# W1 pieces of two batches in shared tile groups, in the banks of the first matmul, and a wider spread of work at the start

## The chip, the cores and the metric

The kernel runs on one core of a Trainium2 chip. The metric is the device time of one execution in microseconds (us); smaller is better. Five engines matter: PE (TensorE, with PEld its weight loads), DVE (VectorE), ACT (ScalarE), POOL (GpSimd) and SP, which here only issues DMAs.

## The reference, cut to what matters

```
# x: (8, 8, 512, 64), state: (8, 8, 32, 64): batch, head, row, width
a     = softmax(x @ state^T / 8);   xread = a @ state      # 512 tokens per batch
a2    = softmax(state @ x^T / 8);   sread = a2 @ x         # 32 tokens per batch
tok   = concat([xread, sread], rows), heads side by side   # 8 x 544 tokens, 512 wide
out   = silu(tok @ w_in) @ w_out                           # w_in 512x2048, w_out 2048x512
```

## The kernel before

The kernel doesn't form `xread`. For each batch it makes W1 = state @ w_in, head by head (256 state rows by 2048 columns), and then multiplies the attention weights with W1. Numbers of `ft` count the 16 slices of 128 hidden columns, `tt` the 4 token tiles of a batch.

```
def w1_mms(b, cols, new=bank):      # one piece: 512 columns of W1, two PSUM banks
    for f, n in cols:
        for hg in range(2):
            pss[f, hg] = new([128, 512], FP32, "ps_w1")
        for s in range(4):
            for hg in range(2):     # 8 matmuls, each in a 64x32 tile of the array
                nc.tensor.matmul(pss[f, hg][ds(32 * s, 32), 0:n], stT[...], w_in_sb[...],
                                 tile_position=(r, 32 * s), ...)

def w1_out(b, cols, engs, pss, at=0):   # eviction: PSUM f32 -> SBUF bf16
    for f, n in cols:
        for hg in range(2):
            copy(engs[hg], W1[b][:, hg, ds(f + at, n)], pss[f, hg][:, ds(at, n)])

# G1(k), emitted by upto(): two 128x512 matmuls W1 x aT into a bank "h1" (two of them),
#   then ACT: g = silu(h).   G2(b, tt, ft): one matmul, out[tt] += g[ft] x w_out[ft]
```

The eight PSUM banks in batch 0 are: o0, o1, a0, a1 for the four outputs; a2, a3 for W1; and two "h1" banks through which all G1 pass in turn. The trace shows PE starting its matmuls in program order, so a G1 that waits for its bank holds up everything behind it. The loop of batch 0:

```
    banks[:] = ["a2", "a3"]
    W0 = {2: (512, 512), 6: (1024, 512), 10: (1536, 512)}
    LEAD0 = [2, 2, 2, 2, 2, 3, 2, 3, 3, 2, 2, 4, 4]
    F3 = 3
    ready = 4
    for ft in range(NFT - 2):
        upto(min(ft + LEAD0[min(ft, 12)], ready))       # G1 ahead of G2
        if ft in W0:
            w1_cols(0, [W0[ft]], both)                  # both = (DVE, ACT)
            ready = sum(W0[ft]) // 128
        ...
        if ft in (5, 9):
            w1_chunks(1, ({5: 0, 9: 1}[ft],), both)     # W1 of batch 1
        ... # ft 11: cast x of batch 1; ft 12: three G2 of tile 3, transposes of x
        for tt in range(4 if ft < F3 else 3):
            G2(0, tt, ft)
    ... # scores and softmax of batch 1, between them the rest of G2;
    ... # near the end the last two W1 pieces of batch 1, in one group
```

The `keep_busy` matmuls at the start are filler: nothing reads their results. Tile 3 has fewer G2 interleaved in the loop (F3); its other G2 are filler for the softmax of batch 1.

The softmax here doesn't subtract the row's maximum and nothing guards it: scores larger than these inputs give would overflow.

Of the kernel before, what the change touches and what calls it, by code (L numbers as in the profile page):

```python
# [25 lines left out]
NFT = DF // 128  # L26
# [15 lines left out]
def kernel(  # L42
# [84 lines left out]
    def cast_x(b, eng, c0=0, nc_=4, h0=0, nh=H):  # L127
        if b < 2:
            x_nat[b] = padded(b)
        elif b not in x_nat:  # L130
            x_nat[b] = xpool.tile([128, 4, 4, 128], BF16, tag="x_nat", name=f"x_nat{b}")
        copy(
            eng,
            x_nat[b][:, ds(c0, nc_), ds(h0 // 2, nh // 2), :].rearrange(
                "p c k (u d) -> p c k u d", u=2
            ),
            x_f[b % 2][:, ds(h0, nh), ds(c0, nc_), :].rearrange("p (k u) c d -> p c k u d", u=2),
        )
# [12 lines left out]
    def load_w_out(g0, n):  # L151
        nc.gpsimd.dma_start(w_out_sb[:, ds(g0, n), :], wout_re[:, ds(g0, n), :])  # L152

    def copy(eng, dst, src):
        if eng is nc.scalar:
            nc.scalar.activation(dst, src, func=COPY, bias=0.0)  # L156
        else:
            eng.tensor_copy(dst, src)  # L158


    def keep_busy(n, pool, tag):
        ps = pool.tile([128, 512], FP32, tag=tag, name="ps_busy")
        for _ in range(n):
            nc.tensor.matmul(  # L164
                ps[:], busy[:, 0:128], busy[:], start=True, stop=True, skip_group_check=True
            )
# [76 lines left out]
    def pe_transpose_x(b, hg, nb=2, new=bank, engs=(nc.vector, nc.scalar), only=None):  # L243
        if b not in xT:
            xT[b] = xtpool.tile([128, 4, 4, 128], BF16, tag="xT", name=f"xT{b}")
        m = 4 // nb
        for u in range(nb) if only is None else only:
            ps = new([128, m, 2, 128], BF16, "ps_xt")
            for i in range(m):
                for j in range(2):  # L250
                    nc.tensor.transpose(  # L251
                        ps[:, i, j, :],
                        x_nat[b][:, m * u + i, 2 * hg + j, :],
                        ident[:],
                    )
            copy(engs[u], xT[b][:, ds(m * u, m), ds(2 * hg, 2), :], ps[:])
# [9 lines left out]
    o_tags = ["o0", "o1"]  # L266
    new_o = lambda sh, dt, nm: psO.tile(sh, dt, tag=o_tags.pop(), name=nm)
    cast_x(0, nc.scalar, 2, 2, 4, 4)
    cast_x(0, nc.gpsimd, 0, 2, 4, 4)
    pe_transpose_x(0, 0, 2, new_o, (nc.vector, nc.vector))  # L270

    st_x = pers.tile([128, 8, B, 4, 2, 2], BF16)

# [116 lines left out]
            aT[b][:, hg, :, :], an[b, hg][:].rearrange("p c s n -> p (c s n)")  # L390
        )

    def pe_transpose_a(b, hg, eng, new=bank, c0=0, n=4):
        ps = new([128, n, 128], BF16, "ps_at")
        for c in range(n):
            nc.tensor.transpose(ps[:, c, :], an[b, hg][:, c0 + c, :, :], ident[:])
        copy(eng, aT[b][:, hg, ds(c0, n), :], ps[:])


    xm_ps = {}  # L400
# [48 lines left out]
    def w1_mms(b, cols, new=bank):  # L449
        pss = {}  # L450
        if b not in W1:
            W1[b] = wpool.tile([128, 2, DF], BF16, tag="W1", name="W1")
# [5 lines that stand above are left out]
                    h = HEAD_OF_SLOT[hg][s]  # L458
                    r = 64 * (h % 2)
                    nc.tensor.matmul(  # L460
                        pss[f, hg][ds(32 * s, 32), 0:n],
                        stT[ds(r, 64), b, h // 2, s % 2, :],
                        w_in_sb[ds(r, 64), h // 2, ds(f, n)],
                        start=True,
                        stop=True,
                        tile_position=(r, 32 * s),
                        skip_group_check=True,
                    )
        return pss

    def w1_out(b, cols, engs, pss, at=0):
# [4 lines that stand above are left out]
    def w1_cols(b, cols, engs, new=bank):  # L476
        w1_out(b, cols, engs, w1_mms(b, cols, new))

    def w1_chunks(b, fbs, engs):
        w1_cols(b, [(512 * fb, 512) for fb in fbs], engs)  # L480
# [83 lines left out]
    def store(b, tt, eng):  # L564
        o = opool.tile([128, DM], FP32, tag="o_sb", name="o_sb")
        copy(eng, o[:], outs[tt][:])
        if b < B:
            nc.sync.dma_start(out_re[ds(136 * b, 128), tt, :], o[:])
        else:
            nc.sync.dma_start(out_sread[ds(512, 32), ds(4 * tt, 4), :], o[:])  # L570
# [21 lines left out]
    def upto(k):  # L592
        while done[0] < min(k, (B + 1) * NFT):
            emit_G1(done[0])
            done[0] += 1

    new_h = lambda sh, dt, nm: psH.tile(sh, dt, tag="h1", name=nm)
    keep_busy(1, psH, "h1")
    scores(0, 0)
    exps(0, 0)  # L600
    keep_busy(1, psH, "h1")
    pe_transpose_x(0, 1, 2, new_h, (nc.vector, nc.scalar))
    norm(0, 0)
    scores(0, 1, 2)
    exps(0, 1)
    norm(0, 1, ((nc.vector, 0, 4),), 2)
    pss0 = w1_mms(0, [(0, 128)])
    nc.scalar.activation(warm[:], busy[:, 0:1], func=SILU, bias=0.0)
    w1_out(0, [(0, 128)], (nc.scalar, nc.scalar), pss0)
    load_w_in(1024)  # L610
    load_w_out(8, 4)
    load_w_in(1536)
    for hg in range(2):
        load_x(1, 4 * hg, 4)
    load_w_out(12, 4)
    load_states()
    load_x(2)
    for i in range(3):
        ones_beside_x(i, nc.gpsimd)
    keep_busy(3, psH, "h1")  # L620
    pss0 = w1_mms(0, [(128, 384)])
    keep_busy(2, psH, "h1")
    new_o = lambda sh, dt, nm: psO.tile(sh, dt, tag=o_tags.pop(), name=nm)
    o_tags[:] = ["o0", "o1"]
    for c in (0, 2):
        pe_transpose_a(0, 0, nc.scalar, new_o, c, 2)
    for c in (0, 2):
        pe_transpose_a(0, 1, nc.vector, bank, c, 2)
    upto(1)
    w1_out(0, [(128, 128)], (nc.vector, nc.vector), pss0)  # L630
    w1_out(0, [(128, 256)], (nc.vector, nc.vector), pss0, 128)
    upto(2)




    banks[:] = ["a2", "a3"]
    turn[0] = 0
    W0 = {2: (512, 512), 6: (1024, 512), 10: (1536, 512)}
    LEAD0 = [2, 2, 2, 2, 2, 3, 2, 3, 3, 2, 2, 4, 4]  # L640
    F3 = 3
    ready = 4
    for ft in range(NFT - 2):
        upto(min(ft + LEAD0[min(ft, 12)], ready))
        if ft in W0:
            w1_cols(0, [W0[ft]], both)
            ready = sum(W0[ft]) // 128
        if ft == 4:
            place_one_state(1, transpose_one_state(st1_n), nc.vector)
        if ft in (5, 9):  # L650
            w1_chunks(1, ({5: 0, 9: 1}[ft],), both)
        if ft == 11:
            for hg in range(2):
                cast_x(1, nc.vector, 0, 4, 4 * hg, 4)
            load_x(3)
        if ft == 12:
            nc.scalar.activation(warm[:], busy[:, 0:1], func=EXP, bias=0.0)
            for i in range(F3, F3 + 3):
                G2(0, 3, i)
            pe_transpose_x(1, 0, 1, engs=(nc.vector,))  # L660
            pe_transpose_x(1, 1, 1, engs=(nc.vector,))
        for tt in range(4 if ft < F3 else 3):
            G2(0, tt, ft)
    F3 += 3
    banks[:] = ["a2", "a3", "a0", "a1"]
    turn[0] = 0
    scores(1, 0, new=new_h)
    scores(1, 1, new=new_h)
    exps(1, 0)
    exps(1, 1)  # L670
    for tt in (0, 2, 1):
        G2(0, tt, 14)
        G2(0, tt, 15)
        if tt != 1:
            store(0, tt, nc.scalar)
    nc.scalar.activation(warm[:], busy[:, 0:1], func=SILU, bias=0.0)
    norm(1, 0)
    norm(1, 1, ((nc.vector, 0, 4),))
    tail_tags = ["a2", "a3", "a0", "o0"]

    def tail_bank(shape, dtype, name):
        tag = tail_tags.pop(0)
        return (psO if tag == "o0" else psA).tile(shape, dtype, tag=tag, name=name)

    for ft in range(F3, NFT):
        if ft == 12:
            pe_transpose_a(1, 0, nc.vector, new_h)
        if ft == 14:
            pe_transpose_a(1, 1, nc.vector, new_h)
            store(0, 1, nc.vector)  # L690
            cols = [(1024, 512), (1536, 512)]
            pss1 = w1_mms(1, cols, tail_bank)
            w1_out(1, cols, (nc.vector, nc.vector), pss1)
            for i in (2, 3):
                for c in range(4):
                    cast_x(i, nc.gpsimd, c, 1)
            transpose_states()
            transpose_x(2)
            upto(NFT + 2)
        G2(0, 3, ft)  # L700
    upto(NFT + 3)
    store(0, 3, nc.vector)

# [100 lines left out]
```

## Time and profile before

| | before |
|---|---|
| median time | 216.54 us (3 runs, 216.5 to 217.24) |
| profiled span | 214.5 us |
| PE busy | 208.0 us, 97% |
| PE's share of the chain that ended last | 87% |
| PE clock granted | 1.0 |

The head of the page of the kernel before, and the chain that ended last:

```profile
span 214.5 us, 3893 instructions
PE 208.0 (97%) x1575; PEld 96.8 (45%) x1575; DVE 76.7 (36%) x170; ACT 139.5 (65%) x244; POOL 39.4 (18%) x61
...
PE 87%; DVE 4%; POOL 3%; ACT 3%; issue 1%; POOLq 0%
```

PE bounds the kernel. Its busy share can't tell how much is left, though: a 128x512 matmul is drawn as 0.38 us long while the next one starts 0.216 us after it, so idle time of up to 0.16 us behind a matmul is drawn as work. Start times tell more. This is the timeline of PE in batch 0 of the kernel before; the columns are start, duration of the merged stretch, engine, line, operation, output<-inputs, array tile, operand size, count, and in brackets the idle time ahead with what ended it:

```profile
12.03 0.60 PE L514 MATMUL h<-aT,W 128*128 128x512 bf16 x2
12.47 0.59 PE L555 MATMUL o<-w_out_sb,g 128*128 128x512 bf16 x2
...
14.83 0.59 PE L514 MATMUL h<-aT,W 128*128 128x512 bf16 x2
15.35 0.41 PE L460 MATMUL ps_w<-w_in_sb,stT 64*32 64x512 bf16 x8
15.69 0.61 PE L555 MATMUL o<-w_out_sb,g 128*128 128x512 bf16 x2
...
27.27 0.38 PE L555 MATMUL o_a<-w_out_sb,g 128*128 128x512 bf16 x1
27.70 1.04 PE L514 MATMUL h<-aT,W 128*128 128x512 bf16 x4
28.99 0.59 PE L514 MATMUL h<-aT,W 128*128 128x512 bf16 x2 [0.25 <-ACT g L546]
...
37.61 0.63 PE L460 MATMUL ps_w<-w_in_sb,stT 64*32 64x512 bf16 x16
38.16 1.04 PE L514 MATMUL h<-aT,W 128*128 128x512 bf16 x4
...
48.30 0.63 PE L303 MATMUL ps_sc<-stT,xT 128*128 128x64 bf16 x16
```

L514 is G1, L555 is G2, L460 is W1. Two G1 matmuls take 0.43 to 0.44 us until the next G2 starts (12.03 to 12.47). Ahead of the W1 group they take 0.52 (14.83 to 15.35), the group of 8 takes 0.34 (15.35 to 15.69), and a group of 16 takes 0.56 (37.61 to 38.16 in the rounded starts). So eight more matmuls in an open group cost 0.22 us and a visit to the tile mode costs some 0.2 us on top. A stall shows as a start that comes too late: from 27.27 to 27.70 is 0.43 us for one matmul of 0.22. Six such stalls can be counted between 12 and 40 us: 0.20 us at 13.32, 0.20 around 20.97, 0.21 at 22.26, 0.22 at 27.70, 0.42 at 28.99 and 0.23 at 36.62. Of these 1.5 us the profile's list of waits shows 0.3.

The first line (12.03) and the last (48.30, the first matmul of batch 2's scores) bound the stretch that the change can alter. It is 36.27 us long; 166.22 us follow.

### The profile page before, as it was taken

The page shows a single profiled execution, that of the slowest core. Times are in us where ns is not written, and L with a number is a line of the kernel's source. Part 1 is how long each engine was busy: PE and PEld are TensorE (multiplying, and loading weights), DVE is VectorE, ACT ScalarE, POOL GpSimd, SP SyncE. Part 2 cuts the span into 40 slices and gives each one's busy share as a digit, 9 for nine tenths or more (in the row PEclk, how much of TensorE's full clock was granted, in tenths as well). Part 3 has the DMA queues.
Part 4 walks back from the last instruction along what each step waited for, and adds up shares of the span by engine and source line. Part 5 has one row for each costly group of instructions (what it writes and reads, how often), then busy time and mean ns, then how long its engine had stood idle before and what let it go on. Part 6 is the DMA issues. An engine that isn't in the chain of part 4 may idle for free.

```text
span 214.5 us, 3893 instructions
## 1 busy us (share of the span) xinstructions
PE 208.0 (97%) x1575; PEld 96.8 (45%) x1575; DVE 76.7 (36%) x170; ACT 139.5 (65%) x244; POOL 39.4 (18%) x61
## 2 busy tenths in 40 slices
PE   7899999999899999999999999999999999999993
PEld 2443344445344444444444444444444444466653
DVE  3733247855951156106610651135312415200011
ACT  3866577699557876699459956886675366644410
POOL 8683013702420212004110402000200000000000
PEclk9999999999999999999999999999999999999999
DMA  6999999795649447464658395115310211011112
GB/s 204 183 205 206 291 267 348 182 234 207 93 101 254 161 107 196 95 201 105 173 74 243 77 151 129 49 52 104 96 51 19 88 49 53 0 49 49 52 49 98
DMA packets 42915, 28.66 MB, mean 134 GB/s; under 512 B 28049, under 2 KB 37777, under 8 KB 42897
## 3 DMA queue, kind: packets, MB, share of 16 engines
q1 hardware_dynamic: 36720, 20.65, 37.0%
q0 software_dynamic: 5888, 7.64, 17.2%
q8 instruction: 12, 0.20, 0.4%
q10 hardware_dynamic: 288, 0.13, 0.2%
q14 instruction: 7, 0.05, 0.1%
HBM read 17.43 MB, written 8.91 MB: 123 GB/s over the span
## 4 chain that ended last, share of the span: by engine, by line
PE 87%; DVE 4%; POOL 3%; ACT 3%; issue 1%; POOLq 0%
PE o L555 47%; PE h L514 26%; PE ps_w L460 4%; PE h L535 3%; PE o_a L555 2%; PE o_part L577 2%; DVE W L158 1%; POOL w_in_sb L149 1%; POOL w_out_sb L152 1%; ACT exp_nat L317 1%; DVE rs L376 1%; PE ps_sr L412 1%; DVE rc L428 1%; PE ps_xt L251 1%; PE ps_scT L329 1%
## 5 line engine op out<-in xcount | busy, mean ns | idle before, releaser
L555 PE MATMUL o<-w_out_sb,g 128*128 128x512 bf16 x496 | 132.2, 379 | 0.0
L546 ACT ACTIVATE g<-h 128x512 bf16<-128x512 f32 (+1 forms) x143 | 81.4, 573 | 37.0 <-PE h L514 23.0
L555 PEld LDWEIGHTS <-g 128*128 128x128 bf16 x528 | 50.0, 98 | 57.6 <-issue 3.2
L514 PE MATMUL h<-aT,W 128*128 128x512 bf16 x254 | 74.8, 379 | 0.4 <-ACT g L546 0.3
L158 DVE COPY o_sb<-o 128x512 f32<-128x512 f32 x15 | 10.4, 691 | 89.1 <-PE o L555 85.2
L514 PEld LDWEIGHTS <-W 128*128 128x128 bf16 x254 | 24.5, 98 | 31.8 <-issue 2.0
L158 DVE CAST W<-ps_w 128x512 bf16<-128x512 f32 (+2 forms) x37 | 23.0, 649 | 25.3 <-PE ps_w L460 25.3
L156 ACT ACTIVATE W<-ps_w 128x512 bf16<-128x512 f32 (+1 forms) x31 | 16.4, 570 | 12.6 <-PE ps_w L460 12.6
L158 POOL CAST x_nat<-x_f 128x512 bf16<-128x512 f32 x24 | 14.5, 647 | 33.3 <-issue 22.5
L156 ACT ACTIVATE o_sb<-o 128x512 f32<-128x512 f32 x16 | 9.6, 597 | 12.1 <-PE o L555 8.9
L359 POOL TENSOR_TENSOR an<-e,rcn 128x512 bf16<-128x512 bf16 x5 | 7.6, 1517 | 49.5 <-DVE rcn L357 49.5
L460 PE MATMUL ps_w<-w_in_sb,stT 64*32 64x512 bf16 (+2 forms) x264 | 11.1, 375 | 0.7 <-DVE W L158 0.7
L555 PE MATMUL o_a<-w_out_sb,g 128*128 128x512 bf16 x32 | 10.2, 379 | 0.0
L535 PE MATMUL h<-xmT,w_in_sb 128*128 128x256 bf16 x64 | 9.6, 273 | 0.0
L535 PEld LDWEIGHTS <-w_in_sb 128*128 128x128 bf16 x64 | 6.3, 98 | 3.9
L164 PE MATMUL ps_busy<-busy 128*128 128x512 bf16 x16 | 6.0, 495 | 1.2 <-DVE warm L171 1.2
L460 PEld LDWEIGHTS <-stT 64*32 64x32 bf16 x264 | 3.4, 89 | 7.3 <-issue 4.9
L748 ACT ACT_TABLE_LOAD x5 | 6.4, 1283 | 0.1
L343 ACT ACTIVATE eT<-ps_scT 128x512 bf16<-128x512 f32 x10 | 5.4, 594 | 1.6 <-PE ps_scT L329 1.6
L379 POOL TENSOR_TENSOR an<-exp_nat,rc 128x512 bf16<-128x512 bf16 x3 | 3.1, 1046 | 18.1 <-ACT eT L343 10.7
L356 DVE TENSOR_REDUCE rs<-e 128x32 f32<-128x1024 bf16 x5 | 6.1, 1211 | 0.2 <-DMA e<-eT 0.2
L108 POOL DMA_DIRECT2D x_f<-in_x_dram x4 | 3.3, 844 | 11.6 <-DVE x_rows L158 9.4
(76 smaller groups left out, 104.4 us busy)
## 6 DMA issues: line engine op xcount, KB each, us to landing
out_dram<-o_sb SPq DMA_DIRECT2D x33, 256.0 KB, 2.4
x_f<-in_x_dram SPq DMA_DIRECT2D x4, 1024.0 KB, 6.2
x_f<-in_x_dram POOLq DMA_DIRECT2D x2, 1024.0 KB, 12.8
w_in_sb<-in_moe_w_in_dram POOLq DMA_DIRECT2D x3, 512.0 KB, 10.0
w_out_sb<-in_moe_w_out_dram POOLq DMA_DIRECT2D x3, 512.0 KB, 11.8
x_f<-in_x_dram SPq DMA_DIRECT2D x2, 512.0 KB, 4.6
x_f<-in_x_dram POOLq DMA_DIRECT2D x2, 512.0 KB, 14.7
w_out_sb<-in_moe_w_out_dram POOLq DMA_DIRECT2D x2, 256.0 KB, 8.0
```

Source lines behind the costliest of these rows:

```text
L156: nc.scalar.activation(dst, src, func=COPY, bias=0.0)
L158: eng.tensor_copy(dst, src)
L164: nc.tensor.matmul(ps[:], busy[:, 0:128], busy[:], start=True, stop=True, skip_group_check=True)
L343: nc.scalar.activation(t[:, hg], scT_ps[hg][:], func=EXP, bias=0.0, scale=SCALE)
L356: nc.vector.tensor_reduce(rs[:], e2[b][:], axis=AX, op=ADD)
L359: eng.tensor_tensor(a[:, hg], e2[b][:, hg], rc[:, hg].to_broadcast([128, 4, 4, NS]), op=MULT)
L460: nc.tensor.matmul(pss[f, hg][ds(32 * s, 32), 0:n], stT[ds(r, 64), b, h // 2, s % 2, :], w_in_sb[ds(r, 64), h // 2, ds(f, n)], start=True, ...
L514: nc.tensor.matmul(h_ps[k][:], W1[b][:, hg, ds(128 * ft, 128)], aT[b][:, hg, :, :], start=(hg == 0), stop=(hg == 1), skip_group_check=True,)
L535: nc.tensor.matmul(ps[:, 0:256], w_in_sb[:, kt, ds(128 * ft, 128)], xmT[:, :, kt].rearrange("p t n b -> p t (n b)"), start=(kt == 0), stop ...
L546: nc.scalar.activation(g[:, 0:n], ps[:, 0:n], func=SILU, bias=0.0)
L555: nc.tensor.matmul(outs[tt][:], gt[b * NFT + ft][:, ds(128 * tt, 128)], w_out_sb[:, ft, :], start=(ft == 0), stop=(ft == NFT - 1), skip_gr ...
L748: nc.scalar.activation(warm[:], busy[:, 0:1], func=SILU, bias=0.0)
```

## The change

Its intent: make batch 1's W1 pieces in the same visits to the tile mode as batch 0's, in the two G1 banks, because W1's own banks are taken; put more G2 of the fourth token tile into the loop; and start sooner by casting x with three engines. The diff, cut to its core:

```diff
-    cast_x(0, nc.gpsimd, 0, 2, 4, 4)
+    cast_x(0, nc.gpsimd, 0, 1, 4, 4)
     pe_transpose_x(0, 0, 2, new_o, (nc.vector, nc.vector))
+    cast_x(0, nc.vector, 1, 1, 4, 4)
@@ start of the attention of batch 0
-    pe_transpose_x(0, 1, 2, new_h, (nc.vector, nc.scalar))
+    pe_transpose_x(0, 1, 2, new_h, (nc.vector, nc.vector))
... (first W1 evictions ahead of the table load; the last load of w_out in two;
...  the aT copies shared by DVE and ACT)
@@ loop of batch 0
-    W0 = {2: (512, 512), 6: (1024, 512), 10: (1536, 512)}
-    LEAD0 = [2, 2, 2, 2, 2, 3, 2, 3, 3, 2, 2, 4, 4]
-    F3 = 3
+    PAIRS = {2: ((512, 512), 0), 6: ((1024, 512), 512), 10: ((1536, 512), 1024)}
+    LEAD0 = [2, 2, 2, 2, 2, 3, 2, 3, 3, 2, 2, 4]
+    F3 = 6
...
-        if ft in W0:
-            w1_cols(0, [W0[ft]], both)
-            ready = sum(W0[ft]) // 128
-        if ft in (5, 9):
-            w1_chunks(1, ({5: 0, 9: 1}[ft],), both)
         for tt in range(4 if ft < F3 else 3):
+            if ft in PAIRS and tt == (2 if ft == 2 else 0):
+                cols, f1 = PAIRS[ft]
+                pss = w1_mms(0, [cols])
+                pss1 = w1_mms(1, [(f1, 512)], new_h)
+                w1_out(0, [cols], both, pss)
+                w1_out(1, [(f1, 512)], both, pss1)
+                ready = sum(cols) // 128
             G2(0, tt, ft)
... (behind the loop: one W1 group of 8 instead of 16, and G2 in another order)
```

Six W1 visits of 8, 8, 8, 8, 8 and 16 matmuls become four of 16, 16, 16 and 8. The number of matmuls stays the same.

More of the change, by code (lines that the diff above doesn't have):

```diff
@@ L391, in transpose_a, with at_mms, pe_transpose_a @@
         )
-    def pe_transpose_a(b, hg, eng, new=bank, c0=0, n=4):
-        ps = new([128, n, 128], BF16, "ps_at")
+    def at_mms(ps, b, hg, c0=0, n=4):
         for c in range(n):
             nc.tensor.transpose(ps[:, c, :], an[b, hg][:, c0 + c, :, :], ident[:])
-        copy(eng, aT[b][:, hg, ds(c0, n), :], ps[:])
+    def pe_transpose_a(b, hg, eng, new=bank):
+        ps = new([128, 4, 128], BF16, "ps_at")
+        at_mms(ps, b, hg)
+        copy(eng, aT[b][:, hg, :, :], ps[:])
     xm_ps = {}
@@ L597 @@
     new_h = lambda sh, dt, nm: psH.tile(sh, dt, tag="h1", name=nm)
+    new_o = lambda sh, dt, nm: psO.tile(sh, dt, tag=o_tags.pop(), name=nm)
     keep_busy(1, psH, "h1")
@@ L606 @@
     norm(0, 1, ((nc.vector, 0, 4),), 2)
-    pss0 = w1_mms(0, [(0, 128)])
+    w1_cols(0, [(0, 128)], (nc.scalar, nc.scalar))
     nc.scalar.activation(warm[:], busy[:, 0:1], func=SILU, bias=0.0)
-    w1_out(0, [(0, 128)], (nc.scalar, nc.scalar), pss0)
     load_w_in(1024)
@@ L614 @@
         load_x(1, 4 * hg, 4)
-    load_w_out(12, 4)
+    load_w_out(12, 2)
+    load_w_out(14, 2)
     load_states()
@@ L620 @@
     keep_busy(3, psH, "h1")
+    banks[:] = ["a2", "a3"]
+    turn[0] = 0
     pss0 = w1_mms(0, [(128, 384)])
     keep_busy(2, psH, "h1")
-    new_o = lambda sh, dt, nm: psO.tile(sh, dt, tag=o_tags.pop(), name=nm)
-    o_tags[:] = ["o0", "o1"]
+    ps_a0 = psO.tile([128, 4, 128], BF16, tag="o1", name="ps_at")
+    at_mms(ps_a0, 0, 0)
+    copy(nc.vector, aT[0][:, 0, 0:2, :], ps_a0[:, 0:2])
+    copy(nc.scalar, aT[0][:, 0, 2:4, :], ps_a0[:, 2:4])
     for c in (0, 2):
-        pe_transpose_a(0, 0, nc.scalar, new_o, c, 2)
-    for c in (0, 2):
-        pe_transpose_a(0, 1, nc.vector, bank, c, 2)
+        ps_a = (psO, psA)[c == 0].tile(
+            [128, 2, 128], BF16, tag=("o0", "a1")[c == 0], name="ps_at"
+        )
+        at_mms(ps_a, 0, 1, c, 2)
+        copy(nc.vector, aT[0][:, 1, ds(c, 2), :], ps_a[:])
+    w1_out(0, [(128, 128)], both, pss0)
     upto(1)
-    w1_out(0, [(128, 128)], (nc.vector, nc.vector), pss0)
     w1_out(0, [(128, 256)], (nc.vector, nc.vector), pss0, 128)
     upto(2)
-    banks[:] = ["a2", "a3"]
     turn[0] = 0
-    W0 = {2: (512, 512), 6: (1024, 512), 10: (1536, 512)}
-    LEAD0 = [2, 2, 2, 2, 2, 3, 2, 3, 3, 2, 2, 4, 4]
-    F3 = 3
+    PAIRS = {2: ((512, 512), 0), 6: ((1024, 512), 512), 10: ((1536, 512), 1024)}
+    LEAD0 = [2, 2, 2, 2, 2, 3, 2, 3, 3, 2, 2, 4]
+    F3 = 6
     ready = 4
-    for ft in range(NFT - 2):
-        upto(min(ft + LEAD0[min(ft, 12)], ready))
-        if ft in W0:
-            w1_cols(0, [W0[ft]], both)
-            ready = sum(W0[ft]) // 128
-        if ft == 4:
+    for ft in range(12):
+        upto(min(ft + LEAD0[ft], ready))
+        if ft == 1:
             place_one_state(1, transpose_one_state(st1_n), nc.vector)
-        if ft in (5, 9):
-            w1_chunks(1, ({5: 0, 9: 1}[ft],), both)
         if ft == 11:
@@ L655 @@
             load_x(3)
-        if ft == 12:
-            nc.scalar.activation(warm[:], busy[:, 0:1], func=EXP, bias=0.0)
-            for i in range(F3, F3 + 3):
-                G2(0, 3, i)
-            pe_transpose_x(1, 0, 1, engs=(nc.vector,))
-            pe_transpose_x(1, 1, 1, engs=(nc.vector,))
-        for tt in range(4 if ft < F3 else 3):
-            G2(0, tt, ft)
-    F3 += 3
-    banks[:] = ["a2", "a3", "a0", "a1"]
-    turn[0] = 0
+        for tt in range(4 if ft < F3 else 3):
+            if ft in PAIRS and tt == (2 if ft == 2 else 0):
[5 more added lines that the diff above has]
+                ready = sum(cols) // 128
+            G2(0, tt, ft)
+    upto(NFT)
+    nc.scalar.activation(warm[:], busy[:, 0:1], func=EXP, bias=0.0)
+    G2(0, 3, 6)
+    pe_transpose_x(1, 0, 1, engs=(nc.vector,))
+    pe_transpose_x(1, 1, 1, engs=(nc.vector,))
+    for ft in range(7, 11):
+        G2(0, 3, ft)
     scores(1, 0, new=new_h)
+    G2(0, 3, 11)
     scores(1, 1, new=new_h)
@@ L670 @@
     exps(1, 1)
-    for tt in (0, 2, 1):
-        G2(0, tt, 14)
-        G2(0, tt, 15)
-        if tt != 1:
-            store(0, tt, nc.scalar)
+    for fts in ((12, 13), (14, 15)):
+        for tt in (0, 2, 1):
+            for ft in fts:
+                G2(0, tt, ft)
+            if fts[1] == 15 and tt != 1:
+                store(0, tt, nc.scalar)
     nc.scalar.activation(warm[:], busy[:, 0:1], func=SILU, bias=0.0)
@@ L678 @@
     norm(1, 1, ((nc.vector, 0, 4),))
-    tail_tags = ["a2", "a3", "a0", "o0"]
-    def tail_bank(shape, dtype, name):
-        tag = tail_tags.pop(0)
-        return (psO if tag == "o0" else psA).tile(shape, dtype, tag=tag, name=name)
-    for ft in range(F3, NFT):
-        if ft == 12:
-            pe_transpose_a(1, 0, nc.vector, new_h)
-        if ft == 14:
-            pe_transpose_a(1, 1, nc.vector, new_h)
-            store(0, 1, nc.vector)
-            cols = [(1024, 512), (1536, 512)]
-            pss1 = w1_mms(1, cols, tail_bank)
-            w1_out(1, cols, (nc.vector, nc.vector), pss1)
-            for i in (2, 3):
-                for c in range(4):
-                    cast_x(i, nc.gpsimd, c, 1)
-            transpose_states()
-            transpose_x(2)
-            upto(NFT + 2)
-        G2(0, 3, ft)
+    pe_transpose_a(1, 0, nc.vector, new_h)
+    G2(0, 3, 12)
+    pe_transpose_a(1, 1, nc.vector, new_h)
+    G2(0, 3, 13)
+    banks[:] = ["a2", "a3", "a0", "a1"]
+    turn[0] = 0
+    w1_cols(1, [(1536, 512)], (nc.vector, nc.vector))
+    store(0, 1, nc.vector)
+    for i in (2, 3):
+        for c in range(4):
+            cast_x(i, nc.gpsimd, c, 1)
+    transpose_states()
+    transpose_x(2)
+    upto(NFT + 2)
+    G2(0, 3, 14)
+    G2(0, 3, 15)
     upto(NFT + 3)
```

## The prediction

> **What bounds the kernel now.** TensorE. The page shows PE busy in 97% of a 214.5 us span and 87% of the chain that ended last, at a granted clock of 1.0. In PE's timeline, matmuls of 512 columns follow each other every 0.216 us from about 12 us on. That agrees with the Trainium skill, page "TensorE: Matmul & The Clock Gate", which gives N/2.4 GHz + 2.5 ns when warm, 215.7 ns. So only two things in batch 0 (12 to 41 us) can be won: stalls, and the cost of entering the 64x32 tile groups that make W1.
>
> Before, from start-to-start times on PE between 12.0 and 40.4 us:
> - six W1 groups. One of 8 matmuls takes 0.34 us plus 0.09 us ahead of it; the double group at 37.6 us takes 0.56 us. So 8 more matmuls in an open group cost 0.22 us and a new group 0.43 us. The skill's page "TensorEngine Tiling (Array Packing)", Key Properties, says that changing the mode drains the array; the trace agrees, at about 0.21 us a visit.
> - stalls of about 1.6 us: 0.2 (bank a1 at 13.3), 0.3 (W1 banks at 20.7), 0.2 and 0.2 (G1 waits for W1 evictions at 22.1 and 27.5), 0.4 (G1 banks at 28 to 29), 0.2 (an at 36.4).
>
> **What the change does.** The matmul count is the same. Three pairs replace five single groups, and the double group at the end becomes single: six visits become four, worth 2 x 0.21 = 0.43 us. The wait for "an" should shrink below 0.1 us, because more G2 work stands ahead.
>
> Against it: batch 1's pieces sit in the two G1 banks, so G1 can't go on until they are evicted. ACT empties two 128x512 PSUM tiles in 1.08 us, DVE in 1.28 us, starting 0.47 us after the group starts. The next G1 can start about 1.6 us after the group's start, while PE has the group (0.56) and two or three G2 (0.43 or 0.65). Estimated stalls: 0.6 after the first pair, 0.4 after the second, and around the third 0.4 (its G1 bank is still held by the SiLU just issued), 0.15, and 0.4 in three G1 in a row: from G1 start to its bank being free takes 1.28 us. With the unchanged 0.2 at the start, stalls are about 2.2 us.
>
> Head: the POOL cast of x (0.68 us) is shared with DVE, so the transposes of the second half start about 0.26 us earlier than 7.22, but the added DVE copy of xT (0.4 us) delays the reductions. I expect the first G1 about 0.1 us earlier.
>
> **Sum:** -0.43 (visits) +0.65 (stalls) -0.1 (head) = about +0.1 us, each term uncertain by 0.2. The change was presumably meant to gain, so I lean slightly below: 216.4 us, 8 in 10 between 215.5 and 217.2. Faster by over 2%: 0.01; within 2%: 0.98; slower: 0.01.
>
> **What would show it.** Three L464 groups of 16 matmuls at about 0.56 us and one of 8; waits "PE h <- ACT W" or "<- DVE W" of 0.4 to 0.6 us after each pair; the last wait for "an" gone; batch 1's first G2 within 0.5 us of 40.4. After that the timelines run parallel.
>
> **What would make it wrong.** Evictions that overlap better than I add up (no G1 stalls: 215.3); a DMA that now comes late (queues are 90% busy until 30 us); a later state transpose, since a store now waits behind the W1 evictions, delaying batch 2's scores at 48 us; a longer head.

## The result, and the profile after

| | before | changed |
|---|---|---|
| median time | 216.52 us (4 runs, 216.31 to 217.24) | 216.88 us (4 runs, 216.83 to 217.08) |
| ratio | | 1.0012, 95% interval 0.9989 to 1.0036 |
| profiled span | 214.5 us | 215.1 us |
| batch 0's second G1 to batch 2's scores | 36.27 us | 36.78 us |
| from there to the end | 166.22 us | 166.20 us |

Ratios here are the mean time of one kernel's fast runs over that of the other's of the same rounds, so not quite the ratio of the medians. The runs alone can't tell the two kernels apart. The traces can: the altered stretch is 0.51 us longer and the rest is the same to 0.02 us. The remaining 0.1 us of the two spans' difference lies ahead of the stretch, where the first load of x landed at 5.09 instead of 4.86 us.

The head of the page of the changed kernel:

```profile
span 215.1 us, 3868 instructions
PE 205.4 (96%) x1549; PEld 96.8 (45%) x1575; DVE 76.6 (36%) x171; ACT 139.6 (65%) x244; POOL 40.0 (19%) x62
```

PE looks 2.6 us less busy, but 26 matmul records are missing from this trace (1549 of 1575), so the two busy sums can't be compared. The timeline of PE in the changed kernel, around the three pairs (L518 is now G1, L559 is G2, L464 is W1):

```profile
12.12 0.60 PE L518 MATMUL h<-aT,W 128*128 128x512 bf16 x2
...
15.93 0.73 PE L464 MATMUL ps_w<-w_in_sb,stT 64*32 64x512 bf16 x16
16.82 0.38 PE L559 MATMUL o_a<-w_out_sb,g 128*128 128x512 bf16 x1 [0.16 <-issue]
17.58 0.59 PE L518 MATMUL h<-aT,W 128*128 128x512 bf16 x2 [0.38 <-ACT W L156]
...
21.98 0.62 PE L464 MATMUL ps_w<-w_in_sb,stT 64*32 64x512 bf16 x16
22.54 0.60 PE L559 MATMUL o<-w_out_sb,g 128*128 128x512 bf16 x2
22.98 0.38 PE L559 MATMUL o_a<-w_out_sb,g 128*128 128x512 bf16 x1
23.63 1.02 PE L518 MATMUL h<-aT,W 128*128 128x512 bf16 x4 [0.27 <-ACT W L156]
...
27.39 0.60 PE L464 MATMUL ps_w<-w_in_sb,stT 64*32 64x512 bf16 x9
28.14 0.41 PE L464 MATMUL ps_w<-w_in_sb,stT 64*32 64x512 bf16 x7 [0.15 <-ACT g L550]
28.48 0.60 PE L559 MATMUL o<-w_out_sb,g 128*128 128x512 bf16 x2
28.92 0.38 PE L559 MATMUL o_a<-w_out_sb,g 128*128 128x512 bf16 x1
29.28 1.02 PE L518 MATMUL h<-aT,W 128*128 128x512 bf16 x4
30.56 0.59 PE L518 MATMUL h<-aT,W 128*128 128x512 bf16 x2 [0.25 <-ACT g L550]
...
48.90 0.63 PE L304 MATMUL ps_sc<-stT,xT 128*128 128x64 bf16 x16
```

The first two pairs are read best from group start to next G1: 15.93 to 17.58 and 21.98 to 23.63, both 1.65 us, although two G2 stand between in the first case (one of their records is missing) and three in the second. The G1 doesn't start when PE gets to it but when its bank is free. ACT and DVE empty the four banks of the pair meanwhile, two each, one after the other. Their timelines in the changed kernel at the first pair, ACT first and then DVE:

```profile
16.44 1.08 ACT L156 ACTIVATE W<-ps_w 128x512 bf16<-128x512 f32 x2 [0.24 <-PE ps_w L464]
```

```profile
16.41 1.29 DVE L158 CAST W<-ps_w 128x512 bf16<-128x512 f32 x2 [1.14 <-PE ps_w L464]
```

ACT ends at 17.52 and the G1 starts at 17.58; after the other two pairs, too, a G1 starts 0.05 us after ACT's second eviction. DVE's second eviction ends later, at 17.70, and so is not what this G1 waits for: the bank that DVE empties goes to the G1 after it. At the third pair PE waits twice more: inside the pair for a G1 bank that a SiLU still reads (28.14), and in the run of three G1 for the SiLU of the first (30.56).

### The profile page after: what moved, and what is told of

It is laid out like the page before. It is cut to its first block, busy times and chain, and to the rows that moved or that the text cites. A ratio compares the mean times of both kernels' runs of the same rounds, so it can differ in the third digit from the quotient of the medians.

```text
span 215.1 us, 3868 instructions
## 1 busy us (share of the span) xinstructions
PE 205.4 (96%) x1549; PEld 96.8 (45%) x1575; DVE 76.6 (36%) x171; ACT 139.6 (65%) x244; POOL 40.0 (19%) x62
## 4 chain that ended last, share of the span: by engine, by line
PE 87%; DVE 5%; ACT 3%; DMA 2%; issue 1%
PE o L559 47%; PE h L518 25%; PE ps_w L464 3%; PE h L539 3%; PE o_a L559 3%; DMA x_f<-in_x_dram 2%; PE o_part L581 2%; DVE rs L377 1%; ACT W L156 1%; ACT g L550 1%; PE ps_sr L416 1%; DVE rc L432 1%; DVE an L380 1%; PE ps_xt L251 1%; PE ps_scT L330 1%
## 5 line engine op out<-in xcount | busy, mean ns | idle before, releaser
L559 PE MATMUL o<-w_out_sb,g 128*128 128x512 bf16 x484 | 129.3, 379 | 1.7 <-issue 0.9
L559 PEld LDWEIGHTS <-g 128*128 128x128 bf16 x528 | 50.2, 98 | 57.9 <-issue 3.2
L518 PE MATMUL h<-aT,W 128*128 128x512 bf16 x243 | 72.4, 379 | 0.9 <-ACT W L156 0.6
L518 PEld LDWEIGHTS <-W 128*128 128x128 bf16 x254 | 24.6, 98 | 32.0 <-issue 2.8
L158 DVE CAST W<-ps_w 128x512 bf16<-128x512 f32 (+2 forms) x35 | 22.1, 659 | 27.0 <-PE ps_w L464 26.9
L156 ACT ACTIVATE W<-ps_w 128x512 bf16<-128x512 f32 (+1 forms) x33 | 17.1, 562 | 12.5 <-PE ps_w L464 12.4
L464 PE MATMUL ps_w<-w_in_sb,stT 64*32 64x512 bf16 (+2 forms) x264 | 11.1, 375 | 1.1 <-DVE W L158 0.7
L559 PE MATMUL o_a<-w_out_sb,g 128*128 128x512 bf16 x30 | 9.9, 379 | 0.4 <-issue 0.2
L464 PEld LDWEIGHTS <-stT 64*32 64x32 bf16 x264 | 3.2, 89 | 7.7 <-issue 5.5
L432 DVE RECIPROCAL rc<-ps_sr 32x2 f32<-32x2 f32 x32 | 5.2, 164 | 0.3
```

Of the source, the lines that this page charges most:

```text
L156: nc.scalar.activation(dst, src, func=COPY, bias=0.0)
L158: eng.tensor_copy(dst, src)
L432: nc.vector.reciprocal(rc[q, :], src)
L464: nc.tensor.matmul(pss[f, hg][ds(32 * s, 32), 0:n], stT[ds(r, 64), b, h // 2, s % 2, :], w_in_sb[ds(r, 64), h // 2, ds(f, n)], start=True, ...
L518: nc.tensor.matmul(h_ps[k][:], W1[b][:, hg, ds(128 * ft, 128)], aT[b][:, hg, :, :], start=(hg == 0), stop=(hg == 1), skip_group_check=True,)
L559: nc.tensor.matmul(outs[tt][:], gt[b * NFT + ft][:, ds(128 * tt, 128)], w_out_sb[:, ft, :], start=(ft == 0), stop=(ft == NFT - 1), skip_gr ...
```

## The experiments

All timed runs have the kernel before in the same rounds: 216.38 us (median of 11 runs, 216.29 to 217.16) for the first four, 216.45 us (11 runs, 216.28 to 217.29) for the last four; the row "changed" is the first comparison, with 216.52 us before. "Stretch" is the time in the trace from batch 0's second G1 to batch 2's first score matmul. All kernels gave correct results.

| kernel | median us | ratio to before, 95% interval | stretch us | after it us |
|---|---|---|---|---|
| before | | | 36.27 | 166.22 |
| changed | 216.88 | 1.0012 (0.9989 to 1.0036) | 36.78 | 166.20 |
| e1_head | 216.32 | 0.9993 (0.9978 to 1.0007) | 36.28 | 166.19 |
| e2_loop | 216.94 | 1.0021 (1.0007 to 1.0036) | 36.78 | 166.21 |
| e3_fill | 214.95 | 0.9926 (0.9910 to 0.9942) | 34.68 | 166.21 |
| e4_split | 215.52 | 0.9956 (0.9940 to 0.9972) | 35.37 | 166.19 |
| e5_order_only | 215.63 | 0.9955 (0.9942 to 0.9968) | 35.42 | 166.20 |
| e6_one_pair | 216.74 | 1.0017 (0.9996 to 1.0038) | 36.44 | 166.22 |
| e7_fill_old_head | 214.74 | 0.9920 (0.9905 to 0.9936) | 34.68 | 166.22 |
| e8_fill_late_chunks | 213.96 | 0.9879 (0.9864 to 0.9895) | 34.69 | 165.33 |

My theory was that the shared visits do save their time and that PE loses more than that behind each pair, waiting for the G1 banks. The rivals were: the head costs it; late weights or evictions that slow other work cost it; or sharing a visit is worth nothing.

### e1_head and e2_loop: the two halves of the change

e1_head has the changed kernel's start (everything up to batch 0's loop) with the old loop; e2_loop the old start with the new loop.

```diff
 e1_head: - loop and end of batch 0 of the changed kernel   + those of the kernel before
 e2_loop: - start of the changed kernel                     + that of the kernel before
```

> Head of the changed kernel (three-engine cast of x, both xT copies on DVE, aT copies shared) with batch 0's loop as before. My theory (head worth little): 0.1 to 0.2 us under the kernel before, first full G1 at 12.0 minus 0.14 us when measured from the landing of the first x load. Rival (the head is what costs the time): 0.3 us or more over the kernel before.

> Head as before, batch 0's loop of the changed kernel. My theory (stalls behind the pairs outweigh the two saved tile-group visits): about 0.5 us over the kernel before, with the same stalls behind the three pairs as in the changed kernel (0.65, 0.43, and 0.5 + 0.15 + 0.4 around the third). Rival (the head costs it): equal to the kernel before or faster.

The loop carries the whole loss: its stretch is 36.78 us under either start, and the old loop's is 36.28 and 36.27. The start's own worth isn't resolved. From the landing of the first x load to the first G1, the ten profiles show 6.2 to 6.7 us for the seven kernels with the new start and 6.4 to 6.7 for the three with the old one; the scatter within one start is larger than the 0.1 us in question. In time, e1_head is within the interval of no difference. Its trace has the first full G1 7.37 us after that landing, against 7.17 in the kernel before, and not the expected 0.14 us sooner.

### e3_fill: the same instructions in another order

G1 runs further ahead before each pair, and five G2 stand behind it before the next G1. Five G2 are 1.08 us, which with the pair's 0.56 makes the 1.64 us until a bank is free.

```diff
-    for ft in range(12):
-        upto(min(ft + LEAD0[ft], ready))
-        ... (the pairs at ft 2, 6, 10; four or three G2 per ft)
+    g2s(3); upto(3); g2s(1); upto(4)        # g2s(n): the next n G2 in the old order
+    place_one_state(1, transpose_one_state(st1_n), nc.vector)
+    g2s(4)
+    pair(512, 0)                            # both pieces and their evictions, as before
+    for n in (5, 2, 1, 1):
+        g2s(n)
+        upto(done[0] + 1)                   # one G1
+    g2s(5)
+    pair(1024, 512)
+    ... (the same four steps; g2s(3); pair(1536, 1024); the casts of x; four steps)
```

> The changed kernel with the same instructions, but batch 0 in another order: G1 runs further ahead before each pair, and five G2 stand between a pair and the next G1. If the pairs cost time only because PE waits for the G1 banks to be emptied, all stalls of batch 0's loop go (2.3 us in the changed kernel's trace) and the time is 214.3 to 215.0 us, faster than both. If the stalls have another cause (late weights, or the evictions slow G2 too), they come back elsewhere and it stays within 0.5 us of the changed kernel.

The stretch shrank by 2.10 us to 34.68, and the time to 214.95 us, 0.7% under the kernel before. The timeline of PE in e3_fill at the first two pairs:

```profile
12.01 0.60 PE L518 MATMUL h<-aT,W 128*128 128x512 bf16 x2
...
15.19 0.87 PE L464 MATMUL ps_w<-w_in_sb,stT 64*32 64x512 bf16 x16
16.00 0.39 PE L559 MATMUL o<-w_out_sb,g 128*128 128x512 bf16 x1
...
20.85 0.63 PE L464 MATMUL ps_w<-w_in_sb,stT 64*32 64x512 bf16 x16
21.41 0.60 PE L559 MATMUL o_a<-w_out_sb,g 128*128 128x512 bf16 x2
21.85 0.59 PE L559 MATMUL o<-w_out_sb,g 128*128 128x512 bf16 x2
22.28 0.38 PE L559 MATMUL o_a<-w_out_sb,g 128*128 128x512 bf16 x1
22.50 0.38 PE L518 MATMUL h<-aT,W 128*128 128x512 bf16 x1
...
46.69 0.63 PE L304 MATMUL ps_sc<-stT,xT 128*128 128x64 bf16 x16
```

From 20.85 to 22.50 it is again 1.65 us from the group to the next G1, but now PE works all the time. Of the stalls in the loop one is left, 0.25 us inside the first pair (15.19 to 16.00 is 0.81 us instead of 0.56); there a weight load of PE waited for DVE to copy batch 1's state, not for a DMA. The same evictions, weights and loads ran closer together and nothing came back elsewhere: the five G2 beside the evictions took 1.09 us (21.41 to 22.50), and no wait of PE for a DMA is listed in the stretch. The rivals of late weights and of evictions that slow other work fall.

PE's busy share of e3_fill reads 96%, as in the changed kernel that is 2 us slower. The Trainium skill, page "Perfetto Trace Analysis", section Identifying Performance Opportunities, calls matmul busy time a bad measure of headroom because pipelined matmuls look smaller in the trace. This pair of runs agrees that the measure is bad, but not with the reason: here a matmul is drawn longer than its pitch, 0.38 us against 0.216.

### e4_split: what a visit costs

One of the five G2 moves in between the two groups of each pair.

```diff
         pss = w1_mms(0, [(f0, 512)])
+        g2s(1)
         pss1 = w1_mms(1, [(f1, 512)], new_h)
...
-    for n in (5, 2, 1, 1):
+    for n in (4, 2, 1, 1):
```

> As e3_fill, with one of the five G2 moved between the two W1 groups of each pair, so that each pair is two visits to the 64x32 tile mode. If a visit costs 0.21 us of PE time that nothing hides, e3_fill plus 3 x 0.21 = 0.6 us. If sharing a visit is worth nothing, the same as e3_fill.

The stretch grew by 0.69 us for three visits more, 0.23 us each, and the time by 0.57 us. The first G1 that bounds the stretch and the scores of batch 2 that end it, in e4_split:

```profile
12.02 0.60 PE L518 MATMUL h<-aT,W 128*128 128x512 bf16 x2
...
47.39 0.63 PE L304 MATMUL ps_sc<-stT,xT 128*128 128x64 bf16 x16
```

The saving that the change was made for is real. The Trainium skill, page "TensorEngine Tiling (Array Packing)", Key Properties, gives the reason as a drain on every change of the tiling mode; these runs show the price and agree with it.

### e5_order_only: the order without the pairs

```diff
-        pss1 = w1_mms(1, [(f1, 512)], new_h)     # G1 banks, same visit
+    def after_it(f1):                            # W1's own banks, a visit of its own
+        g2s(4); upto(done[0] + 1); g2s(3)
+        single(1, f1)                            # w1_cols(1, [(f1, 512)], both)
+        for n in (0, 1, 1):
+            g2s(n); upto(done[0] + 1)
```

> The order of e3_fill without the pairing: each W1 piece of batch 1 has a visit of its own in W1's own two banks, as in the kernel before, and no piece is in a G1 bank. Seven visits instead of four. If only shared visits matter once the order is good: e3_fill plus 3 x 0.21 = 0.6 us, about 215.5, the same as e4_split. If holding the G1 banks still costs something hidden in e3_fill, it is faster than e4_split; if the pairs were what made the gain, it is near the kernel before, 216.4.

It equals e4_split: a stretch of 35.42 against 35.37 us, with seven visits each. The same two lines in e5_order_only:

```profile
12.32 0.61 PE L518 MATMUL h<-aT,W 128*128 128x512 bf16 x2
...
47.75 0.63 PE L304 MATMUL ps_sc<-stT,xT 128*128 128x64 bf16 x16
```

So, with enough work behind the pair, holding the G1 banks costs nothing; and of the 1.59 us by which e3_fill's stretch is under that of the kernel before, 0.85 us (36.27 - 35.42) come from the order alone (with one visit more than the six of the kernel before, which could have had this order), and 0.74 us from sharing three visits.

### e6_one_pair: one stall taken away

```diff
-        upto(min(ft + LEAD0[ft], ready))
+        if ft != 3:
+            upto(min(ft + LEAD0[ft], ready))
...
+            if (tt, ft) == (3, 3):
+                upto(min(ft + LEAD0[ft], ready))
             G2(0, tt, ft)
```

> The changed kernel with one thing moved: the G1 behind the first pair comes three G2 later. My theory: the stall of 0.65 us behind the first pair goes, some 0.1 to 0.2 us comes back at the first G2 that needs this G1's SiLU; 0.4 to 0.6 us faster than the changed kernel, all other stalls as they are. If the stall is not made by the G1's wait for its bank, it stays and the time is 216.9.

The stretch is 0.34 us shorter than in the changed kernel, the time only 0.14 us (216.74 against 216.88, from different rounds, so not resolved). The timeline of PE in e6_one_pair:

```profile
16.27 0.73 PE L464 MATMUL ps_w<-w_in_sb,stT 64*32 64x512 bf16 x16
16.93 0.61 PE L559 MATMUL o_a<-w_out_sb,g 128*128 128x512 bf16 x2
17.38 0.59 PE L559 MATMUL o<-w_out_sb,g 128*128 128x512 bf16 x2
17.81 0.38 PE L559 MATMUL o_a<-w_out_sb,g 128*128 128x512 bf16 x1
18.02 0.59 PE L518 MATMUL h<-aT,W 128*128 128x512 bf16 x2
18.46 0.38 PE L559 MATMUL o_a<-w_out_sb,g 128*128 128x512 bf16 x1
18.67 0.59 PE L518 MATMUL h<-aT,W 128*128 128x512 bf16 x2
19.31 0.60 PE L559 MATMUL o<-w_out_sb,g 128*128 128x512 bf16 x2
```

The stall behind the pair is gone: five G2 follow without a gap up to the G1 at 18.02. But I had expected 0.4 to 0.6 us, and missed. Of the 0.65 us, 0.1 us lies inside the group (0.66 instead of 0.56; in the changed kernel 0.67 once its missing record is allowed for) and stayed, and 0.2 us came back at 19.31, where the first G2 that needs this G1's SiLU starts 0.64 instead of 0.43 us after the G1 before it. A later G1 fills the hole behind the pair and opens one ahead of its own reader. e3_fill avoids that by having run G1 further ahead.

### e7_fill_old_head: the start again

```diff
 e3_fill, - start of the changed kernel   + start of the kernel before
```

> The loop of e3_fill under the head of the kernel before. If the new head is worth 0.1 us as predicted: 0.0 to 0.2 us slower than e3_fill. If the head matters, 0.3 us or more.

The stretch is the same, 34.68 us, and the time 214.74 us against 214.95; the intervals of the two ratios overlap almost wholly. If the new start is worth anything it is under what these runs resolve, and no run shows a gain from it.

### e8_fill_late_chunks: a better kernel

```diff
-                    if at == (2, 8):
+                    if at == (2, 12 if b == 1 else 8):
                         w1_chunks(n, (2, 3), both)
```

> e3_fill, and in batch 1 the last two W1 pieces of batch 2 are made four G2 later, where PE waited 0.7 us for their banks because DVE was busy with the state readout. Expected: that wait goes, 0.6 to 0.7 us faster than e3_fill, 214.3 us. A try for a better kernel; it bears on the change only as a second case of PE waiting for an eviction.

It is the fastest, 213.96 us, 1.2% under the kernel before. The part after the stretch is 0.88 us shorter than in e3_fill, somewhat more than expected: PE had waited 0.68 us by the list of waits, and more by start times, because the drawn length of the matmul ahead hides some of it. The timeline of PE at this place, e3_fill first and then e8_fill_late_chunks:

```profile
55.16 0.41 PE L464 MATMUL ps_w<-w_in_sb,stT 64*32 64x512 bf16 x8
56.24 0.41 PE L464 MATMUL ps_w<-w_in_sb,stT 64*32 64x512 bf16 x8 [0.68 <-DVE W L158]
56.59 2.12 PE L559 MATMUL o<-w_out_sb,g 128*128 128x512 bf16 x9
```

```profile
56.16 0.64 PE L464 MATMUL ps_w<-w_in_sb,stT 64*32 64x512 bf16 x16
56.73 1.25 PE L559 MATMUL o<-w_out_sb,g 128*128 128x512 bf16 x5
```

The two groups took 1.43 us (55.16 to 56.59) and take 0.57 us now.

## Why the prediction was right

The predicted 216.4 us and the measured 216.88 us differ by 0.5 us, inside the range; "within 2%" held, which asks little where the two terms in question are under 1 us (0.5%) each. What counts is the mechanism, point by point:

- *PE bounds it, and only stalls and visits can change.* Right. The stretch ahead of batch 2 took all of the change, and the remaining 166.2 us stayed the same.
- *Two visits saved, 0.21 us each.* Right. e4_split shows 0.23 us a visit, e5_order_only 0.25.
- *New stalls behind the pairs.* Right in place and cause, low in size. Counted as start-to-start time less the same work unhindered, with the prediction in brackets: first pair 0.65 (0.6), second 0.43 (0.4), inside the third 0.53 (0.4), behind it 0.14 (0.15), in the three G1 0.42 (0.4), bank a1 at the start 0.2 (0.2), the wait for "an" 0.1 (under 0.1). That is 2.47 us instead of the 2.2 predicted. A bank was free 1.65 us after the group started, not 1.6.
- *The start 0.1 us sooner.* Not confirmed: below the scatter of 0.5 us between profiles, and neither e1_head nor e7_fill_old_head resolves it.
- *The sum, +0.1 us.* The trace's stretch is +0.51 us. With the measured terms: +0.99 of stalls (2.47 - 1.48) and -0.46 for two visits make +0.53 us, which places all of it. The mis-sized terms are the growth of the stalls, predicted +0.65, and the start, which I had counted as a gain. The growth was low at both ends: the new stalls are 2.47 us and not 2.2, and those of the kernel before, counted the same way, are 1.48 us and not 1.6 (the wait for the W1 banks at 20.7 is 0.2 us, not 0.3).
- *"The change was presumably meant to gain, so I lean slightly below."* This step was wrong. It moved the answer 0.2 us away from the sum, in the wrong direction, on no evidence of the profile.
- *What would make it wrong.* A missing DMA or a late state transpose played no part: the part behind the stretch didn't change.

The expected gain of the shared visits is there and was spent: about 0.46 us won, about 0.99 us lost as the stalls grew. The new waits came from too little work between a pair and the next G1, as e3_fill shows, and not from sharing a visit.

## What to carry to other kernels

When work moves into PSUM banks that a running pipeline uses, count the time until the bank that is needed first has been evicted (here 1.65 us from the group's start: 0.51 until ACT's first eviction starts, 1.08 for its two evictions, and 0.05 until the G1) and put that much independent work behind it; also run the pipeline further ahead, or the hole only moves to the next reader. The Trainium skill points the same way in page "TensorEngine Tiling (Array Packing)", section PSUM Bottleneck: tiling speeds up the matmuls and not the emptying of PSUM; here both ACT and DVE were already used for it, and the order decided. Read stalls on an almost full PE from start-to-start times, because the profile draws a matmul longer than its place in the queue and hides short gaps.

## What the Trainium skill lacked or had wrong

- "TensorE: Matmul & The Clock Gate", section Back-to-back issue gap, gives about 131 ns per 512-column matmul as the sustained rate of a stream of weight loads and matmuls, and calls N/2.4 + 2.5 ns (216 ns) too high there. Here such a stream of full-array matmuls, a weight load ahead of each, never ran under 215 ns from one start to the next in any of the ten traces, at a granted clock of 1.0.
- "TensorEngine Tiling (Array Packing)", section Key Properties, says that a change of tiling mode drains the array but gives no price. Here a visit to the 64x32 mode between full-array matmuls cost 0.23 to 0.25 us beside its matmuls (e4_split and e5_order_only against e3_fill), and eight more matmuls in an open visit 0.22 us.
- "ScalarE: Activation LUTs", section What ACT_TABLE_LOAD costs, adds a drain of about 1.38 us to the load of 1.28 us. In these traces the load takes 1.28 us, starts 0.02 us after the activation ahead of it and is followed by the next one within 0.02 us (in the changed kernel the load starts at 9.49 and the activation at 10.79), so no such drain is seen on either side.
- "Perfetto Trace Analysis", section Identifying Performance Opportunities, says that matmul busy time misleads, because pipelined matmuls look smaller in the trace, but not how far a gap is hidden. Here they look longer: a 0.38 us matmul record at a pitch of 0.216 us hides up to 0.16 us of each stall, and the list of waits showed 0.3 of about 1.5 us.
